# Plain instead of seven-fold products for one token block of the second expert, with a longer list of planner refinements

## The chip, the cores and the metric

One core of one Trainium2 chip. The metric is the device time of the kernel in microseconds (us). Before the change it is 1051.25 us, the median of three runs (1050.07 to 1051.81). The engines are named as in the profile: PE (TensorE, matmul), PEld (its weight loads), DVE (VectorE), ACT (ScalarE), POOL (GpSimd), SP (SyncE, which here issues the DMAs).

## The reference, cut to what matters

```python
def reference(**kw):                          # all float32
    attn = _attn_ref(q, k, v, s)              # q, k, v: (4, 8, 576, 64), causal, with a position bias from s
    x = attn.transpose(0, 2, 1, 3).reshape(2304, 512)
    h = x @ moe_w_in                          # 512 -> 2048, first expert
    x = (h - np.tanh(h)) @ moe_w_out          # 2048 -> 512
    a, b = x @ moe2_w_a, x @ moe2_w_b         # 512 -> 1536 each, second expert
    return (a * b) @ moe2_w_out               # 1536 -> 512, output (2304, 512)
```

## The kernel before, in words

Three stages follow one another and overlap: attention, the first expert in nine token blocks of 256, and the second expert in five token blocks, the first of 256 tokens and four of 512.

Every float32 operand is split into two 16-bit halves (high and low), and a product of two operands is three matmuls: high by high, high by low, low by high (`PROD`).

The second expert has 2304 tokens, 512 inputs and 1536 = 6 x 256 = 12 x 128 hidden columns. There are two ways to compute a block:

- **Plain** (`l3_mm`, `l3_act`, `l4_mm`; only the block of 256 tokens before the change). For each of the 12 tiles f of 128 hidden columns, 12 matmuls give a, 12 give b, ACT scales b into a tile `th`, DVE multiplies a by it into `g`, the result is split into `ghl` (the high half is a copy on ACT, DVE or POOL, the low half an operation on DVE or POOL), and `l4_mm` accumulates three matmuls of 512 columns for each 128 tokens into the `acc` banks.
- **Seven** (`seven`, `seven_act`, `seven_out`; the four blocks of 512). For each of the 6 chunks of 256 columns the 2x2 block product over (input halves, token halves) is done by seven instead of eight smaller products: 84 matmuls of 256 columns for a and b together and 24 of 512 columns for the output. It needs sums of token operands, five per block (`b_sums`), and sums of weight parts, five per chunk for a and b together, 30 in all (`a_sums`). One sum is three additions and a split: three operations on DVE or POOL, one copy on ACT, DVE or POOL, one subtraction on DVE or POOL. The results of `a_sums` lie in the space of the first expert's weights (`w1`, through `a_place`), so they can't be made before the first expert has used those; they are read from `w2`, the second expert's split weights. The intermediate values of `a_sums` lie in the buffers named `xf`, of which there are two (`XF = 2`), given out strictly in the order of the program (fifo); one buffer serves two sums, so the 30 sums take 15 in turn, and the first result buffer of `b_sums` comes behind them in the same order.

`blocks2` says which chunks are seven: block and chunk are counted through (block x 6 + chunk), and a chunk of a 512 block is seven from the number `SEVEN` on. With `SEVEN = 6` all of block 1 is seven.

The order of the instructions on each engine is not written out by hand. All operations are first recorded with their dependencies, a price in ns (`cost`) and a due time (`due`); a list scheduler (`Plan.run`) then walks a modelled time, and each engine takes the ready operation with the earliest due time whose buffers are free. Where an operation may run on several engines (`either`), `best` compares the modelled end times, with the prices of DVE multiplied by `WV` (attention and first expert) or `WV2` (second expert) and those of POOL by `WP`. Before the final run, `refine` performs one step for each entry of `REFINE`: it runs the model, computes how late each operation could start (`backward`), and moves the due times part of the way towards that, with random shifts from a seed. The engines then execute each queue in the fixed order that results: an instruction that waits holds up all behind it on its engine.

One line of the profile, L544, stands for nearly every instruction, since all are recorded through one helper; they are told apart by their tiles. `h`, `qk`, `acc` and `pv` are PSUM banks (2, 3, 2 and 1 of them). `pv` is also used for small sums, among them that of `x2_cols`, whose result DVE writes to `y1` (named y in the profile).

Of the kernel before, what the change touches and what calls it, by code (L numbers as in the profile page):

```python
# [3 lines left out]

# [29 lines left out]
MASKED = -1.0e34  # L34
BLOCKS = [(p, [b]) for p in range(2) for b in range(4)]
TURN = 0.0
REFINE = [(200.0, 0.2, 300.0, 242), (200.0, 0.2, 1000.0, 199), (0.0, 0.1, 0.0, 21), (100.0, 0.0, 1000.0, 484), (100.0, 0.05, 0.0, 139), (200.0, 0.2, 1000.0, 988), (400.0, 0.05, 300.0, 648), (0.0, 0.0, 1000.0, 437), (0.0, 1.0, 300.0, 81)]
SEVEN = 6
SUMSTEP = 20e3
XF = 2  # L40
WS = 2
# [3 lines left out]
PART1 = 60e3  # L45
TAILS = 100e3
SLACK = 0.0
WV = 1.1
WP = 1.2
WV2 = 1.1  # L50
N = None
ORDER1 = [7, 6, 5, 4, 7, 6, 5, 7, 6, 7, 6, N, N, N, N, N]
ORDER2 = [8, 7, 6, 5, N, N, 8, 7, 6, N, N, 8, 7, 8, N, N, N, N]
# [126 lines left out]


class Op:
    __slots__ = ("eng", "fn", "dur", "dl", "succ", "wait", "ready", "bufs", "seq", "lag", "size", "what", "alts", "done", "pred", "end", "part", "cost", "lock")


class Plan:
# [52 lines left out]
    def record(self, eng, fn, reads, writes, keys_r, keys_w, dur, lag, size, shift=0.0, alts=None):  # L239
        for part in (self.parts, self.alts):  # L240
            if part is not None:
                part.append((eng, fn, reads, writes, keys_r, keys_w, dur, lag, size, shift))
                return
        op = Op()
        op.eng, op.fn, op.dur, op.dl = eng, fn, dur, self.due + shift
        op.part = self.due, eng == "sync"
        op.cost = self.cost
        op.succ, op.wait, op.ready, op.seq = [], 0, 0.0, len(self.ops)
        op.lag, op.size = lag, size
        op.alts, op.done = alts or [(eng, fn, dur, lag)], False  # L250
        op.what = getattr(fn, 'what', '')
        op.bufs = []
        before = set()
        for kind, views in (("r", reads), ("w", writes)):
            for v in views:
                b = v.buf
                m = v.mask()
                assert kind == "w" or not b.fresh, b.name
                b.fresh = False
                if b not in op.bufs:  # L260
                    op.bufs.append(b)
                for p0, p1, hm, ho in b.wrote:
                    if hm & m and p0 < v.p1 and v.p0 < p1 and ho is not op:
                        before.add(ho)
                if kind == "r":
                    b.seen.append((v.p0, v.p1, m, op))
                    continue
                rest = []
                for h in b.seen:
                    p0, p1, hm, ho = h  # L270
                    if hm & m and p0 < v.p1 and v.p0 < p1:
                        if ho is not op:
                            before.add(ho)
                        if not hm & ~m and v.p0 <= p0 and p1 <= v.p1:
                            continue
                    rest.append(h)
                b.seen = rest
                b.wrote = [h for h in b.wrote if h[2] & ~m or h[0] < v.p0 or h[1] > v.p1]
                b.wrote.append((v.p0, v.p1, m, op))
        for v in self.hold:  # L280
            if v.buf not in op.bufs:
                op.bufs.append(v.buf)
        self.hold = ()
        for k in keys_r:
            before.update(self.keys.get(k, []))
        for o in before:
            o.succ.append(op)
        op.pred = list(before)
        op.wait = len(before)
        for k in keys_w:  # L290
            self.keys.setdefault(k, []).append(op)
        self.ops.append(op)

    def begin(self):

        self.open = {}
        self.unused = {}
        for t in self.tags.values():
            t["next"] = t["live"] = 0
        seen = set()  # L300
        for op in self.ops:
            op.wait, op.ready, op.done = len(op.pred), 0.0, False
            for b in op.bufs:
                if b not in seen:
                    seen.add(b)
                    b.left, b.real = 0, None
                    self.unused[b.pool] = self.unused.get(b.pool, 0) + 1
                b.left += 1
# [70 lines left out]
    def run(self, switch=None):  # L379
# [4 lines left out]
        ready = {e: [] for e in engines}  # L384
# [5 lines left out]

        def offer(op):
            for a in op.alts:
                heapq.heappush(ready[a[0]], (op.dl, op.seq, op))

        def best(op, e):
            mine = [a for a in op.alts if a[0] == e][0]
            least = mine[2] * op.cost.get(e, 1.0) + (max(port - now, 0.0) if mine[1].lock else 0.0)
            for a in op.alts:
                if a is not mine:
                    t = max(free[a[0]] - now, 0.0, port - now if a[1].lock else 0.0) + a[2] * op.cost.get(a[0], 1.0)  # L400
                    for dl, seq, o in ready[a[0]]:
                        if dl < op.dl and len(o.alts) == 1:
                            t += o.dur
                    if t < least:
                        return None
            return mine
# [12 lines left out]
        n = 0  # L419
        while left:  # L420
            moved = True
            while moved:
                moved = False
                for e in order():
                    if free[e] > now or not ready[e]:
                        continue
                    put, op = [], None
                    late = False
                    while ready[e]:
                        x = heapq.heappop(ready[e])  # L430
                        if x[2].done:
                            continue
                        way = x[2].alts[0] if len(x[2].alts) == 1 else best(x[2], e)
                        if way and self.fits(x[2], switch):
                            if not way[1].lock or port <= now:
                                op = x[2]
                                break
                            late = True
                        put.append(x)
                        if len(put) > 200:  # L440
                            break
                    for x in put:
                        heapq.heappush(ready[e], x)
                    if op is None:
                        if late:
                            n += 1
                            heapq.heappush(events, (port, n + 0.7, 1, None))
                        continue
                    for b in op.bufs:
                        if b.real is not None:  # L450
                            continue
                        t = self.tags[b.pool, b.tag]
                        t["live"] += 1
                        t["next"] = max(t["next"], b.nth + 1)
                        b.real = switch is None or self.open[b.pool].tile(
                            b.shape, b.dtype, tag=b.tag, name=b.name, bufs=t["bufs"])
                    op.eng, op.fn, op.dur, op.lag = way
                    op.done = True
                    op.lock = op.fn.lock
                    if op.lock:  # L460
                        port = now + op.dur
# [10 lines left out]
                    if e == "sync":  # L472
                        dma = max(dma, now + op.dur + 650.0) + op.size
                        end = dma
# [12 lines left out]
            now, _, kind, op = heapq.heappop(events)  # L487
            batch = [(kind, op)]
            while events and events[0][0] <= now:
                _, _, kind, op = heapq.heappop(events)  # L490
# [33 lines left out]
class _Eng:  # L524
# [3 lines left out]
    def __getattr__(self, what):  # L528
        plan, name = self.plan, self.name

        def call(*args, reads=(), writes=(), **kw):
            rd, wr = [], []
            for i, a in enumerate(args):
                if isinstance(a, View):
                    (wr if i == 0 else rd).append(a)
            for k, a in kw.items():
                if isinstance(a, View):
                    (wr if k in ("out", "accum_out") else rd).append(a)
            def real(a):
                assert not isinstance(a, View) or a.buf.real is not None, (name, what, a.buf.name, a.buf.tag)  # L540
                return a.real() if isinstance(a, View) else a

            def fn():
                getattr(getattr(plan.nc, name), what)(  # L544
                    *[real(a) for a in args], **{k: real(a) for k, a in kw.items()})

            fn.what = (name, what)
            fn.lock = shares(name, what, rd, wr)
            dur, lag, size = cost(name, what, rd, wr, kw, args)
            plan.record(name, fn, rd, wr, reads, writes, dur, lag, size, plan.shift.get(name, 0.0))  # L550

        return call
# [72 lines left out]
def tile_attention_two_moes(  # L625
# [22 lines left out]
    NF2 = F2 // P  # L648
# [974 lines left out]
    pl.vector.tensor_scalar(out=y2, in0=y1, scalar1=fin, scalar2=2.0 ** 43, op0=ALU.mult, op1=ALU.mult)  # L1623
    t0 = start[-1]
    todo = blocks2()
    t1 = t0 + NF2 * 36 * todo[0]["n"] / 2.4
    for i, c in enumerate(dict.fromkeys(c for blk in todo for c in blk["seven"])):
        due(t1 + (i - 3) * SUMSTEP)
        a_sums(c)
# [69 lines left out]
```

## Time and profile before

| | before |
|---|---|
| median of three runs | 1051.25 us |
| the profiled execution's own time | 1052.22 us |
| its span | 1050.4 us |
| PE busy | 922.6 us, 88% |
| DVE busy | 876.7 us, 83% |
| ACT busy | 545.1 us, 52% |
| POOL busy | 129.2 us, 12% |
| mean granted PE clock | 0.967 |

The span is the time from the first to the last instruction of the profiled execution; 1.8 us of that execution's own time lie around it. Busy times are shares of the span; an engine can bound one stretch and idle in another, so the stretches have to be looked at one by one. Of the granted clock, 1.00 is 2.4 GHz and 0.50 is 1.2 GHz.

### The profile page before, as it was taken

How to read it: one execution, taken by the hardware profiler on the slowest of the kernel's cores; microseconds unless marked ns; L12 is line 12 of the kernel's file. 1: busy time of each engine (PE TensorE's matmuls, PEld its weight loads, DVE VectorE, ACT ScalarE, POOL GpSimd, SP SyncE). 2: the span in 40 equal slices, each digit the busy share in tenths (PEclk: the TensorE clock that was granted, in tenths of full speed). 3: DMA queues.
4: the chain of work that ended last, by engine and by line, in shares of the span. 5: the costliest groups of instructions: out<-in, count | busy, mean ns of one | idle time of the engine just before them, and what ended most of it. 6: DMA issues, size and time to landing. Idle time of an engine off the chain costs nothing.

```text
span 1050.4 us, 21289 instructions
## 1 busy us (share of the span) xinstructions
PE 922.6 (88%) x8214; PEld 715.1 (68%) x8214; DVE 876.7 (83%) x2178; ACT 545.1 (52%) x1106; POOL 129.2 (12%) x194
## 2 busy tenths in 40 slices
PE   1698689997998989998898898169999999999998
PEld 0476578885777667777787785057777777777775
DVE  8899899798998999996999899999569559655555
ACT  6797766667777677874967443222222222212211
POOL 3120411013322332510000010000000000000000
PEclk9999899999999999999899998679999999999999
DMA  9999756378997988957735310010011002001001
GB/s 240 236 287 231 186 126 105 50 157 161 190 182 143 179 168 161 188 125 170 295 121 161 101 41 1 0 51 31 2 41 41 1 1 80 1 1 42 1 1 41
DMA packets 282086, 113.98 MB, mean 109 GB/s; under 512 B 251200, under 2 KB 265776, under 8 KB 281984
## 3 DMA queue, kind: packets, MB, share of 16 engines
q1 hardware_dynamic: 281984, 112.62, 46.3%
q8 instruction: 64, 1.05, 0.4%
q14 instruction: 38, 0.31, 0.1%
HBM read 60.53 MB, written 11.17 MB: 68 GB/s over the span
## 4 chain that ended last, share of the span: by engine, by line
PE 35%; DVE 14%; DMA 5%; ACT 3%; issue 1%; SPq 0%; DVEq 0%; ACTq 0%
PE h L544 13%; PE qk L544 9%; PE acc L544 8%; PE pv L544 5%; DVE xf L544 5%; DVE w L544 2%; ACT w L544 2%; DMA xf<-in_moe_w_out_dram 1%; DMA xhl<-x_d 1%; DVE ghl L544 1%; DVE x2f L544 1%; DVE x2hl L544 1%; DMA w<-in_moe_w_b_dram 1%; DVE g L544 1%; DMA w<-in_moe_w_a_dram 1%
## 5 line engine op out<-in xcount | busy, mean ns | idle before, releaser
L544 PEld LDWEIGHTS <-w 128*128 128x128 f16 x5376 | 526.2, 99 | 147.7 <-issue 33.1
L544 PE MATMUL h<-xhl,w 128*128 128x256 f16 x2256 | 281.4, 276 | 1.0 <-DVE xhl L544 1.0
L544 PE MATMUL acc<-ghl,w 128*128 128x256 f16 x1536 | 195.1, 277 | 9.9 <-DVE ghl L544 3.8
L544 PE MATMUL h<-xf,w 128*128 128x256 f16 (+1 forms) x704 | 103.6, 297 | 1.8 <-DVE w L544 1.5
L544 DVE TENSOR_TENSOR g<-g,h 128x512 f32<-128x512 f32 x48 | 32.8, 684 | 51.6 <-PE h L544 50.7
L544 DVE CUSTOM_DVE_ANT_0 qk<-qk,caus,cs 128x384 f32<-128x384 f32 (+2 forms) x120 | 64.4, 554 | 5.0 <-PE qk L544 4.6
L544 ACT ACTIVATE qk<-qk,nm 128x384 f32<-128x384 f32 (+2 forms) x120 | 59.8, 498 | 15.8 <-DVE nm L544 9.3
L544 PE MATMUL qk<-qkT 128*128 128x128 f16 (+4 forms) x168 | 46.8, 320 | 23.4 <-DVE a L544 14.0
L544 PEld LDWEIGHTS <-qkT 128*128 128x128 f16 (+2 forms) x352 | 29.3, 103 | 54.7 <-issue 32.4
L544 DVE SCALAR_TENSOR_TENSOR a<-qk,sm,a 128x384 f16<-128x384 f32 (+3 forms) x120 | 62.9, 547 | 4.0 <-ACT a L544 3.9
L544 PEld LDWEIGHTS <-ghl 128*128 128x128 f16 x360 | 35.2, 98 | 39.2 <-DVE ghl L544 2.7
L544 ACT ACTIVATE th<-pv 128x256 f32<-128x256 f32 x24 | 9.2, 383 | 94.9 <-PE pv L544 89.8
L544 ACT ACTIVATE sq<-h 128x512 f32<-128x512 f32 x48 | 28.5, 595 | 56.9 <-PE h L544 55.4
L544 ACT ACTIVATE th<-h,xc 128x512 f32<-128x512 f32 x64 | 43.8, 684 | 25.2 <-PE h L544 23.8
L544 ACT ACTIVATE ghl<-h,xsg 128x512 f16<-128x512 f32 x57 | 39.1, 685 | 30.0 <-DVE h L544 28.9
L544 DVE SCALAR_TENSOR_TENSOR h<-h,xc,th 128x512 f32<-128x512 f32 x64 | 48.1, 752 | 7.3 <-ACT th L544 6.9
L544 PE MATMUL acc<-w,ghl 128*128 128x512 f16 x216 | 52.1, 381 | 2.2 <-DVE ghl L544 2.2
L544 PEld LDWEIGHTS <-sq 128*128 128x128 f16 (+1 forms) x306 | 29.7, 98 | 35.0 <-POOL sq L544 2.0
L544 DVE SCALAR_TENSOR_TENSOR ghl<-h,xsg,ghl 128x512 f16<-128x512 f32 x64 | 47.5, 743 | 3.1 <-ACT ghl L544 2.9
L544 PE MATMUL qk<-kB,qkT 67*128 67x128 f16 (+4 forms) x168 | 46.3, 318 | 1.7 <-DMA kB<-part_d 1.6
L544 PEld LDWEIGHTS <-v 128*64 128x64 f16 x1440 | 37.8, 112 | 14.0 <-issue 13.4
L544 ACT ACTIVATE sq<-raw 128x576 bf16<-128x576 f32 (+2 forms) x57 | 38.6, 678 | 15.1 <-DMA raw<-tail_d 6.8
(243 smaller groups left out, 1683.5 us busy)
## 6 DMA issues: line engine op xcount, KB each, us to landing
w<-in_moe_w_out_dram SPq DMA_DIRECT2D x8, 1024.0 KB
w<-in_moe_w_in_dram SPq DMA_DIRECT2D x6, 1024.0 KB
x_d<-x2hl SPq DMA_DIRECT2D x18, 256.0 KB
raw<-in_k_dram SPq DMA_DIRECT2D x32, 128.0 KB
raw<-in_v_dram SPq DMA_DIRECT2D x32, 128.0 KB
w<-in_moe_w_a_dram SPq DMA_DIRECT2D x4, 1024.0 KB
xhl<-x_d SPq DMA_DIRECT2D x4, 1024.0 KB
out_dram<-x2f SPq DMA_DIRECT2D x16, 256.0 KB
```

The costliest lines, as they stand in the source:

```text
L544: getattr(getattr(plan.nc, name), what)(*[real(a) for a in args], **{k: real(a) for k, a in kw.items()})
```

## The change

Block 1 of the second expert becomes plain (`SEVEN` goes from 6 to 12), so blocks 2 to 4 are seven. The due times of the weight sums are moved behind all plain blocks together, where they lay behind block 0. The weights of DVE in the choice between engines rise (`WV` 1.1 to 1.3, `WV2` 1.1 to 1.2). `REFINE` has 26 steps where it had 9, none of them kept. The planner's ready queues become sorted lists in place of heaps, with the same order of due time and number, and its prices are rounded to whole ns.

```diff
-REFINE = [(200.0, 0.2, 300.0, 242), (200.0, 0.2, 1000.0, 199), (0.0, 0.1, 0.0, 21),
...
+REFINE = [(2000.0, 0.1, 300.0, 180), (2000.0, 0.2, 0.0, 123), (2000.0, 0.1, 300.0, 60),
...
-SEVEN = 6
+SEVEN = 12
...
-WV = 1.1
+WV = 1.3
 WP = 1.2
-WV2 = 1.1
+WV2 = 1.2
...
         def offer(op):
             for a in op.alts:
-                heapq.heappush(ready[a[0]], (op.dl, op.seq, op))
+                insort(ready[a[0]], (op.dl, op.seq, op))
...
                     for dl, seq, o in ready[a[0]]:
-                        if dl < op.dl and len(o.alts) == 1:
-                            t += o.dur
+                        if dl >= op.dl or t >= least:
+                            break
+                        if len(o.alts) == 1:
+                            t += o.alts[0][2]
...
-            dur, lag, size = cost(name, what, rd, wr, kw, args)
+            dur, lag, size = map(round, cost(name, what, rd, wr, kw, args))
...
     todo = blocks2()
-    t1 = t0 + NF2 * 36 * todo[0]["n"] / 2.4
+    t1 = t0 + NF2 * 36 / 2.4 * sum(blk["n"] for blk in todo if not blk["seven"])
     for i, c in enumerate(dict.fromkeys(c for blk in todo for c in blk["seven"])):
         due(t1 + (i - 3) * SUMSTEP)
         a_sums(c)
```

## Rows read from the trace of the kernel before

**Rows 1.** The page: busy time of each engine, and PE and DVE in 40 slices.
```profile
PE 922.6 (88%) x8214; PEld 715.1 (68%) x8214; DVE 876.7 (83%) x2178; ACT 545.1 (52%) x1106; POOL 129.2 (12%) x194
...
PE   1698689997998989998898898169999999999998
...
DVE  8899899798998999996999899999569559655555
```

**Rows 2.** Busy time by stretch: length, engines (instructions), granted clock, DMA.
```profile
45.00:140.00 95.00, 73.79 (x441) 57.56 (x441) 88.35 (x265) 74.34 (x144) 22.80 (x27) 0.95 0.95 243
140.00:250.00 110.00, 105.10 (x1045) 88.27 (x1042) 99.70 (x314) 72.92 (x180) 16.74 (x33) 1.00 0.57 110
250.00:480.00 230.00, 208.22 (x2574) 164.62 (x2573) 213.37 (x627) 174.11 (x387) 63.94 (x106) 0.99 0.88 166
480.00:605.50 125.50, 112.86 (x1046) 96.63 (x1040) 111.28 (x251) 79.53 (x107) 9.79 (x8) 0.95 0.51 168
605.50:660.00 54.50, 51.31 (x386) 38.66 (x383) 53.02 (x98) 21.17 (x42) 2.53 (x2) 0.93 0.06 20
660.00:690.40 30.40, 0.04 (x2) 0.03 (x2) 30.40 (x53) 8.71 (x14) 0.00 (x0) 0.57 0.00 0
690.40:789.00 98.60, 98.04 (x732) 72.58 (x733) 75.16 (x136) 25.24 (x47) 2.59 (x3) 0.98 0.11 33
...
877.00:963.00 86.00, 85.94 (x647) 63.18 (x646) 57.23 (x100) 20.14 (x38) 0.00 (x0) 1.00 0.04 13
```

**Rows 3.** PE in order of time: start, length, instructions, idle time before and releaser.
```profile
643.30 1.20 PE L544 MATMUL acc<-w,ghl 128*128 128x512 f16 x4 [2.25 <-DVE ghl L544]
645.43 2.72 PE L544 MATMUL pv<-xhl,w 128*128 128x256 f16 x12 [0.94 <-DVE bits L544]
647.95 2.77 PE L544 MATMUL h<-xhl,w 128*128 128x256 f16 x12
650.51 1.64 PE L544 MATMUL acc<-w,ghl 128*128 128x512 f16 x6
...
690.38 2.74 PE L544 MATMUL pv<-xhl,w 128*128 128x256 f16 x12 [30.36 <-DVE y L544]
693.68 2.22 PE L544 MATMUL pv<-xhl,w 128*128 128x256 f16 x12 [0.56 <-ACT th L544]
695.74 1.47 PE L544 MATMUL h<-xhl,w 128*128 128x256 f16 x12
697.05 1.46 PE L544 MATMUL acc<-w,ghl 128*128 128x512 f16 x6
698.34 1.47 PE L544 MATMUL h<-xf,w 128*128 128x256 f16 x12
```

**Rows 4.** DVE in order of time, around the end of the weight sums.
```profile
684.49 1.88 DVE L544 SCALAR_TENSOR_TENSOR w<-xf,w 128x512 f16<-128x512 f32 x3
686.29 0.68 DVE L544 SCALAR_TENSOR_TENSOR xf<-x2hl,xf 128x512 f16<-128x512 f32 x1
...
690.11 0.21 DVE L544 TENSOR_SCALAR y<-pv,xik 128x2 f32<-128x2 f32 x1
```

**Rows 5.** Groups of DVE instructions from 597 to 690 us: busy, mean ns, idle before.
```profile
L544 DVE TENSOR_TENSOR xf<-w 128x512 f32<-128x512 f16 x60 | 38.8, 679 | 0.0
L544 DVE TENSOR_TENSOR xf<-xf 128x512 f32<-128x512 f32 x30 | 20.3, 678 | 0.0
L544 DVE SCALAR_TENSOR_TENSOR w<-xf,w 128x512 f16<-128x512 f32 x29 | 19.4, 679 | 0.0
```

**Rows 6.** Windows of 10 us: the last of the gap.
```profile
680.00:690.00 10.00, 0.00 (x0) 0.00 (x0) 10.00 (x18) 2.87 (x5) 0.00 (x0) 0.50 0.00 0
```

**Rows 7.** Groups from 640 to 730 us: a 512-column scaling on ACT, a multiplication on DVE.
```profile
L544 ACT ACTIVATE bits<-h,cpc 128x512 f32<-128x512 f32 x2 | 1.4, 687 | 1.3 <-PE h L544 1.3
L544 DVE TENSOR_TENSOR bits<-h,bits 128x512 f32<-128x512 f32 x2 | 1.4, 680 | 0.0
```

**Rows 8.** Groups of DVE instructions up to 605 us: the largest group of copies.
```profile
L544 DVE TENSOR_SCALAR a<-qk,sm 128x512 f16<-128x512 f32 x13 | 9.7, 743 | 0.0
```

More of the change, by code (lines that the diff above doesn't have):

```diff
@@ L1 @@
 import heapq
+from bisect import bisect_left, insort
 import random
@@ L36 @@
 TURN = 0.0
-REFINE = [(200.0, 0.2, 300.0, 242), (200.0, 0.2, 1000.0, 199), (0.0, 0.1, 0.0, 21), (100.0, 0.0, 1000.0, 484), (100.0, 0.05, 0.0, 139), (200.0, 0.2, 1000.0, 988), (400.0, 0.05, 300.0, 648), (0.0, 0.0, 1000.0, 437), (0.0, 1.0, 300.0, 81)]
-SEVEN = 6
+REFINE = [(2000.0, 0.1, 300.0, 180), (2000.0, 0.2, 0.0, 123), (2000.0, 0.1, 300.0, 60), (100.0, 0.0, 300.0, 89760), (2000.0, 0.05, 300.0, 21221), (100.0, 0.3, 0.0, 973), (100.0, 0.05, 0.0, 783), (2000.0, 0.3, 2000.0, 579), (0.0, 0.1, 300.0, 477), (-200.0, 0.0, 300.0, 45834), (0.0, 0.1, 1000.0, 331), (0.0, 0.1, 1000.0, 12795), (2000.0, 0.05, 300.0, 56244), (-200.0, 0.1, 300.0, 44216), (0.0, 0.7, 2000.0, 938), (0.0, 0.1, 2000.0, 6594), (-200.0, 0.0, 1000.0, 66042), (200.0, 0.5, 1000.0, 11562), (200.0, 0.2, 0.0, 26092), (100.0, 0.2, 1000.0, 96071), (400.0, 0.1, 0.0, 92832), (-200.0, 0.05, 2000.0, 89277), (400.0, 0.0, 3000.0, 30568), (200.0, 0.05, 2000.0, 84539), (100.0, 0.05, 300.0, 64962), (-200.0, 0.1, 0.0, 21270)]
+SEVEN = 12
 SUMSTEP = 20e3
@@ L182 @@
 class Op:
-    __slots__ = ("eng", "fn", "dur", "dl", "succ", "wait", "ready", "bufs", "seq", "lag", "size", "what", "alts", "done", "pred", "end", "part", "cost", "lock")
+    __slots__ = ("eng", "fn", "dur", "dl", "succ", "wait", "ready", "bufs", "seq", "lag", "size", "what", "alts", "pred", "end", "part", "cost", "lock")
 class Plan:
@@ L249, in record @@
         op.lag, op.size = lag, size
-        op.alts, op.done = alts or [(eng, fn, dur, lag)], False
+        op.alts = alts or [(eng, fn, dur, lag)]
         op.what = getattr(fn, 'what', '')
@@ L301, in begin @@
         for op in self.ops:
-            op.wait, op.ready, op.done = len(op.pred), 0.0, False
+            op.wait, op.ready = len(op.pred), 0.0
             for b in op.bufs:
@@ L426, in run @@
                         continue
-                    put, op = [], None
+                    op = None
                     late = False
[L429 to L432, printed above, removed]
+                    for x in ready[e][:201]:
                         way = x[2].alts[0] if len(x[2].alts) == 1 else best(x[2], e)
@@ L438, in run @@
                             late = True
[L439 to L443, printed above, removed]
                     if op is None:
@@ L448, in run @@
                         continue
+                    for a in op.alts:
+                        del ready[a[0]][bisect_left(ready[a[0]], (op.dl, op.seq))]
                     for b in op.bufs:
@@ L457, in run @@
                     op.eng, op.fn, op.dur, op.lag = way
-                    op.done = True
                     op.lock = op.fn.lock
```

## The prediction, made before the changed kernel was run

> **What bounds the kernel now.** I read the page's busy shares and slices first. No engine is full over the span: PE 88%, DVE 83%. But PE's slices show one hole, a 1 followed by a 6 at about 656 to 710 us, while DVE's slices there are all 9 [rows 1]. The windows put it exactly: from 660.0 to 690.4 us PE does nothing (0.04 us) and DVE is busy for all 30.40 us. Before it, from 45 to 605.5 us, DVE is busy for 512.7 of 560.5 us and PE for 500.0; behind it PE is full, 98.04 of 98.60 us in block 1 and 85.94 of 86.00 in a later block, with DVE at 57 of 86 [rows 2]. So there are three regimes: DVE and PE close together up to 605, DVE alone from there to the end of the hole, PE alone from there on.
>
> The view of PE in order of time tells what ends the hole: 30.36 us before the matmuls into `pv` at 690.38, released by DVE's y [rows 3]. That is `y1`, at 690.11 on DVE, behind the weight sums and the first token sums of block 1 [rows 4]. It waits for no data: `x2_cols` was done long before. It is only placed late in DVE's queue. The deeper cause is what stands in front of it: from 597 to 690 us DVE does 60 + 30 + 29 = 119 operations of `a_sums`, with no idle time before any of them [rows 5]. Three of them in a row start 1.80 us before the next one, 0.60 us each [rows 4], so they take 119 x 0.60 = 71.4 us. Block 1 can't begin without them: its `b_sums` result lies in an `xf` buffer, and the fifo gives it out after the 15 of the weight sums. Had `y1` come early, PE would have finished block 0 and then waited all the same.
>
> **The change part by part.** The sum is made against the profiled execution (1052.22 us, span 1050.4); the median is 1.0 below that execution, and I apply the difference to the median.
>
> *The hole.* Plain block 1 needs neither `a_sums` nor `b_sums`, so PE can go from block 0 straight into it. Gone: 30.36 us, and the 0.56 us of the next wait [rows 3]; 30.9 us.
>
> *The clock behind the hole.* In the last 10 us of the hole the granted clock is 0.50, the lower level, 1.2 GHz [rows 6]. The first two groups of 12 matmuls behind it take 2.74 (against 1.47) and 693.68 to 695.74 = 2.06 us (against 695.74 to 697.05 = 1.31) [rows 3]: 1.27 + 0.75 = 2.0 us, gone too.
>
> *The small stall ahead of it.* At 640 to 650 us PE waits 2.25 us for a `ghl` and 0.94 us for `bits`, both from a DVE full of sums, and its next 24 matmuls run slow: 645.43 to 650.51 = 5.08 against 2.62 us [rows 3]. Together 5.65 us. The sums' due times now lie behind both plain blocks, so they should step back behind `ghl`. But DVE takes whatever is ready, and the model may still let a sum go first. Bounds 0 and 5.65; I take half, 2.8 us.
>
> *More matmul work in block 1.* 12 matmuls of 256 columns take 1.31 us, 0.109 each; 6 of 512 take 697.05 to 698.34 = 1.29 us, 0.215 each [rows 3]. Seven: a chunk is 84 x 0.109 + 24 x 0.215 = 14.3 us, six are 86.0 (the later block of rows 2 shows 85.94). Plain: 12 tiles x 36 x 0.215 = 92.9 us. Added, all of it on PE's path: 6.9 us. Nothing hides it, since PE is the bound from here on.
>
> *Block 1's own chain.* A plain tile needs a scaling on ACT (0.69), a multiplication on DVE (0.68) [rows 7], a copy and a subtraction, each like these: about 2.7 us. PE has the next tile's 24 matmuls of 512 columns meanwhile, 5.2 us, with `h`, `g` and `ghl` double. I cost it at nothing; without that cover it would be 2.7 us for each of 12 tiles, 32 us.
>
> *Are the sums done in time for block 2?* They are moved and not removed; the fifo of `xf` means that block 2 needs all 30 before its `b_sums`. From 605.5 us on DVE has 83.4 us of work that it did up to 690.4 [rows 2], 12 tiles x (2 x 0.60 + a copy of at most 0.60) = 21.6 for the plain block, 20 x 0.60 = 12.0 for the `b_sums` of block 2, and I allow 10 for what stood behind the hole (`y1`, the last split, the output of block 0): 127 us. PE has the 51.3 us that it did between 605.5 and 660 [rows 2] and 92.9 of plain block, 144 us. So the sums are hidden, with some 17 us to spare, and what comes next is limited by PE, as block 2 is already. If that cover is gone, the `b_sums` stand open: 12 us. SP's queue has little in it here (DMA share 0.06 and 0.11 in these stretches [rows 2]); block 2's tokens are loaded when block 0 gives back its buffer, long ahead.
>
> This cover hangs on the 0.60 us. The Trainium skill (VectorE: DVE Perf Modes, "The DRAIN you can't avoid") says that the next operation on DVE doesn't start before the pipe of the one ahead is empty. Taken at its word, a sum's operation costs its full 0.68 us [rows 5], and 163 operations would add 13 us: 140 of 144, hardly any cover left. The trace has starts 0.60 apart with lengths of 0.68 to 0.69 [rows 4], so a tail of 0.08 us overlaps; the measurement decides, and the sum above stands.
>
> *Everything before 605 us.* New refinement steps, `WV` 1.3 and rounded prices reorder every queue there. None of this removes work; PE's work up to 605 us is unchanged. What it can win is idle time: 60.5 us on PE, 47.8 us on DVE from 45 us on, with ACT idle for 159.6 of 560.5 us [rows 2]. `WV` pushes copies towards ACT; the largest group of such copies on DVE has 9.7 us [rows 8], and DVE is the fuller engine. Bounds: a third of PE's idle time at best, -20 us; on the other side a plan that is worse by as much as one small stall in each of two places, +11. I take -6, a tenth of PE's idle time. From 605.5 on, `WV2` touches only a DVE that is not the bound.
>
> Sum: -30.9 - 2.0 - 2.8 + 6.9 - 6 = -34.8, from 1051.25 to 1016.4; I say 1016 us.
>
> **The rivals.**
> (a) The order before 605 us wins far more, 15 to 20 us: 1002 to 1007. For it: ACT's 160 idle us and DVE's lead. Against: DVE is at 91% there, and PE at 89%, both must be fed at once.
> (b) It loses up to 11 us: up to 1033. For it: the whole order is drawn anew, by a model and not by this trace.
> (c) Block 2 waits for its token sums: 1016 + 12 = 1028. For it: the fifo. Against: 17 us of spare.
> (d) The hole stays: `y1` is again queued behind the sums, since the new due times are as free to put it there. Then nothing but -6 and +6.9 is left: 1052. Against: the sums now have later due times, and plain tiles behind `pv` give the model a price for a late `y1`, which it hadn't while block 1 waited anyway.
> (e) Slower: the hole is cut up and spread. In block 1 each of the 12 tiles needs DVE twice, in a queue that is full of sums. Where a tile's `ghl` comes late, as at 640 us, PE stands and then runs at 1.2 GHz: 5.65 us a time, of which 2.46 is clock [rows 3]. All 12 tiles: 12 x 5.65 = 67.8, 1084 us; from seven such stalls on (7 x 5.65 = 39.6 against 34.8) the kernel is slower than before. For it: DVE is over 97% busy from 605.5 to 660 [rows 2]. Against: in that same stretch PE was busy for 51.31 of 54.5 us [rows 2] with block 0, whose tiles have half the matmuls for cover. The Trainium skill (TensorE: Matmul & The Clock Gate, "HAM oscillation") describes this, a clock lost again at each repeated wait, so that many short gaps can cost more than one long one; the stall at 640 us agrees, 3.19 us of waiting followed by 2.46 us of slow matmuls.
>
> **How the numbers follow.** Forecast 0.58, with its own range 1007 to 1026; (a) 0.13; (b) 0.12; (c) 0.09; (d) 0.04; (e) 0.04. (a), (b) and (c) are faster like the forecast, 0.92; I count (d) half as no change and half as slower: 0.92 faster, 0.02 same, 0.06 slower. A difference below 0.2% (2.1 us) can't be told from none. The range takes in (c), nearly all of (b) and most of (a): 1001 to 1033.
>
> **What would show it.** Right: no PE idle time over 5 us between 600 and 1000 us; the granted clock at 0.9 or more in each window of 10 us from 610 on; block 1 as 12 x 36 matmuls of 512 columns in about 93 us; weight sums on DVE beside them, the last of them before block 1 ends; the three seven blocks at 86 us each. The part before 605 us is right if the point that is at 605.5 us in the windows before (where the last weights of the second expert are split and its first matmuls start) comes between 592 and 604 us. Wrong: a wait of PE for `y`, `ghl` or token sums of 10 us or more in total behind 605; or a start of the second expert that moves by more than 15 us either way.

## The result, and the profile after

| | before | after |
|---|---|---|
| median (lowest to highest) | 1051.53 us (1050.07 to 1054.76), 4 runs | 1019.39 us (1017.87 to 1020.79), 4 runs |
| profiled execution: time, span | 1052.22, 1050.4 us | 1020.0, 1018.2 us |
| mean granted PE clock | 0.967 | 0.987 |

The ratio is 0.969, with a 95% interval of 0.9663 to 0.9717: 32 us faster. 1016 us was predicted, with a range of 1001 to 1033.

The page of the changed kernel, busy time of each engine and the slices of PE and DVE; it answers to [rows 1].
```profile
PE 921.8 (91%) x7998; PEld 691.8 (68%) x7998; DVE 831.4 (82%) x2084; ACT 546.7 (54%) x1101; POOL 140.9 (14%) x201
...
PE   1688789998877888899999999999999999999998
...
DVE  7799999879989999999799999999456659545554
```
The 1 and the 6 in PE's slices are gone: from the 18th slice on (433 us), each but the last is a 9. DVE's busy time fell by 45 us and PE's by 0.8, so PE's share rose to 91% by the shorter span alone.

Windows of the changed kernel: length, then busy time (instructions) of PE, weight loads, DVE, ACT, POOL, granted clock, DMA share, GB/s. The first six have the bounds of [rows 2]; then come the rest of block 1, the first seven block, and all behind 605.5 us.
```profile
45.00:140.00 95.00, 76.70 (x455) 60.65 (x454) 86.91 (x265) 79.67 (x149) 15.56 (x21) 0.93 0.87 229
140.00:250.00 110.00, 104.05 (x1035) 87.03 (x1033) 94.88 (x298) 74.83 (x184) 20.59 (x31) 1.00 0.61 119
250.00:480.00 230.00, 199.14 (x2422) 156.59 (x2423) 215.04 (x599) 159.36 (x354) 69.32 (x108) 0.97 0.87 161
480.00:605.50 125.50, 120.63 (x1212) 104.82 (x1211) 114.18 (x271) 92.16 (x135) 10.97 (x10) 1.00 0.59 180
605.50:660.00 54.50, 52.90 (x418) 40.32 (x416) 54.43 (x109) 23.21 (x47) 2.42 (x2) 1.00 0.07 20
660.00:690.40 30.40, 30.40 (x142) 13.81 (x141) 30.39 (x52) 10.75 (x19) 1.16 (x1) 1.00 0.22 70
690.40:746.00 55.60, 55.60 (x259) 25.25 (x258) 35.27 (x60) 10.29 (x16) 0.00 (x0) 1.00 0.00 1
746.00:832.00 86.00, 85.78 (x644) 62.71 (x642) 52.61 (x93) 21.57 (x40) 6.22 (x5) 1.00 0.08 26
...
605.50:1018.20 412.70, 406.21 (x2796) 272.89 (x2793) 282.83 (x500) 109.67 (x200) 16.55 (x14) 1.00 0.07 24
```
The stretch from 660.0 to 690.4, in which PE did nothing [rows 2], is full on PE *and* on DVE. The last line is everything behind 605.5 us; the same view of the kernel before reads:
```profile
605.50:1050.40 444.90, 406.91 (x3032) 298.38 (x3029) 324.79 (x569) 113.99 (x213) 7.11 (x6) 0.96 0.07 22
```
These two lines hold the result. The stretch is shorter by 444.9 - 412.7 = 32.2 us, the whole difference of the spans (1050.4 - 1018.2), as it must be when both are cut at the same moment; what tells is what fills it. PE's idle time in it falls from 38.0 to 6.5 us, by 31.5; its busy time hardly moves (-0.7). From 45 to 605.5 us PE's idle time is 60.5 us before [rows 2] and, by the first four windows above, 560.5 - 500.5 = 60.0 after.

PE in order of time in the changed kernel (start, length, instructions, in brackets the idle time before and its releaser), answering to [rows 3]:
```profile
606.53 0.16 PE L540 MATMUL pv<-wac,ones 128*128 128x1 bf16 x1 [0.59 <-ACT xf L540]
...
610.66 2.67 PE L540 MATMUL acc<-ghl,w 128*128 128x256 f16 x23 [0.97 <-DVE ghl L540]
613.17 1.47 PE L540 MATMUL qk<-xhl,w 128*128 128x256 f16 x12
...
644.99 2.75 PE L540 MATMUL qk<-xhl,w 128*128 128x512 f16 x12
...
659.34 2.75 PE L540 MATMUL h<-xhl,w 128*128 128x512 f16 x12
...
704.67 2.75 PE L540 MATMUL qk<-xhl,w 128*128 128x512 f16 x12
707.26 2.75 PE L540 MATMUL h<-xhl,w 128*128 128x512 f16 x12
...
743.52 2.75 PE L540 MATMUL pv<-xhl,w 128*128 128x512 f16 x12
746.11 1.47 PE L540 MATMUL h<-xf,w 128*128 128x256 f16 x12
```
The first product of block 1 (512 columns, from `xhl`) starts at 644.99, between tiles of block 0; from 659.34 to the first product of block 2 at 746.11 no group has a bracket: no wait. The last outputs of block 0 fall into this stretch, and those of the last three tiles of block 1 behind it. Twelve such matmuls take 707.26 - 704.67 = 2.59 us, so block 1's 12 x 36 cost 36 x 2.59 = 93.2 us.

DVE in order of time in the changed kernel, answering to [rows 4], and its groups of the sums from 597 to 750 us, answering to [rows 5]:
```profile
646.45 0.21 DVE L540 TENSOR_SCALAR y<-pv,xik 128x2 f32<-128x2 f32 x1
...
701.90 0.69 DVE L540 SCALAR_TENSOR_TENSOR w<-xf,w 128x512 f16<-128x512 f32 x1
702.50 0.69 DVE L540 TENSOR_TENSOR g<-h,th 128x512 f32<-128x512 f32 x1
703.11 1.29 DVE L540 SCALAR_TENSOR_TENSOR w<-xf,w 128x512 f16<-128x512 f32 x2
704.31 0.69 DVE L540 SCALAR_TENSOR_TENSOR ghl<-g,ghl 128x512 f16<-128x512 f32 x1
...
705.51 0.69 DVE L540 SCALAR_TENSOR_TENSOR w<-xf,w 128x512 f16<-128x512 f32 x1
...
720.15 0.68 DVE L540 SCALAR_TENSOR_TENSOR w<-x2hl,w 128x512 f16<-128x512 f32 x1
```
```profile
L540 DVE TENSOR_TENSOR xf<-w 128x512 f32<-128x512 f16 x59 | 39.3, 701 | 0.0
L540 DVE SCALAR_TENSOR_TENSOR w<-xf,w 128x512 f16<-128x512 f32 x29 | 19.3, 685 | 0.0
L540 DVE TENSOR_TENSOR xf<-xf 128x512 f32<-128x512 f32 x29 | 19.2, 685 | 0.0
```
There are 117 operations of weight sums where there were 119: they are moved, not removed. The plain block's `g` and `ghl` now stand between them, one pair to a tile. The last weight sum is at 705.51, the last token sum of block 2 at 720.15, ended 25 us ahead of block 2's first product (746.11 - 720.83). And `y1` comes at 646.45, 44 us earlier.

### The profile page after: what moved, and what is told of

It reads as the page before. It is cut to its first block, busy times and chain, and to the rows that moved or that the text cites. A ratio compares the mean times of both kernels' runs of the same rounds, so it can differ in the third digit from the quotient of the medians.

```text
span 1018.2 us, 20791 instructions
## 1 busy us (share of the span) xinstructions
PE 921.8 (91%) x7998; PEld 691.8 (68%) x7998; DVE 831.4 (82%) x2084; ACT 546.7 (54%) x1101; POOL 140.9 (14%) x201
## 4 chain that ended last, share of the span: by engine, by line
PE 50%; DVE 23%; DMA 12%; ACT 8%; issue 5%; SPq 2%; POOL 0%; DVEq 0%; ACTq 0%; POOLq 0%
PE h L540 19%; PE acc L540 13%; PE qk L540 12%; PE pv L540 6%; DMA qkT<-qk 5%; DVE qk L540 4%; DVE a L540 3%; DVE w L540 3%; SPq L540 2%; ACT sq L540 2%; DVE g L540 2%; ACT w L540 2%; DVE h L540 1%; DVE ghl L540 1%; DMA w<-in_moe_w_in_dram 1%
## 5 line engine op out<-in xcount | busy, mean ns | idle before, releaser
L540 PEld LDWEIGHTS <-w 128*128 128x128 f16 x5160 | 500.8, 98 | 135.4 <-issue 28.3
L540 PE MATMUL h<-xhl,w 128*128 128x256 f16 (+1 forms) x2256 | 296.8, 283 | 7.0 <-DVE ghl L540 3.3
L540 PE MATMUL h<-xf,w 128*128 128x256 f16 (+1 forms) x560 | 85.9, 304 | 1.0 <-ACT xf L540 0.8
L540 ACT ACTIVATE qk<-qk,nm 128x384 f32<-128x384 f32 (+3 forms) x120 | 59.9, 499 | 35.9 <-DVE nm L540 23.6
L540 DVE CUSTOM_DVE_ANT_0 qk<-qk,caus,cs 128x384 f32<-128x384 f32 (+3 forms) x120 | 64.7, 555 | 4.0 <-PE qk L540 3.1
L540 PE MATMUL acc<-w,ghl 128*128 128x512 f16 x252 | 60.6, 379 | 0.0
L540 ACT ACTIVATE sq<-h 128x512 f32<-128x512 f32 x36 | 21.4, 596 | 60.2 <-PE h L540 58.7
L540 DVE TENSOR_TENSOR g<-sq 128x256 f32<-128x256 f32 x35 | 14.4, 422 | 47.4 <-ACT sq L540 47.3
L540 ACT ACTIVATE w<-w 128x1024 f32<-128x1024 f32 (+1 forms) x42 | 48.2, 1158 | 6.4 <-DMA w<-in_moe_w_a_dram 2.4
L540 DVE TENSOR_TENSOR g<-g,h 128x512 f32<-128x512 f32 x36 | 24.5, 685 | 27.4 <-PE h L540 26.2
```

The costliest lines, as they stand in the source:

```text
L540: getattr(getattr(plan.nc, name), what)(*[real(a) for a in args], **{k: real(a) for k, a in kw.items()})
```

## Experiments

Each ratio is against the kernel before, run on the same chip. Two theories stand against each other. *The hole*: the sums that block 1 needs, 71 us of DVE work, are what PE waited for, and the plain block is what removes the wait. *The order*: the hole is an accident of one queue (`y1` behind the sums), and the refined order, not the plain block, is what removes it.

### One part at a time, each with its old or new plan

**e1_block_alone**: the plain block in the kernel before; its refinement steps, weights and planner stay.
```diff
-SEVEN = 6
+SEVEN = 12
-    t1 = t0 + NF2 * 36 * todo[0]["n"] / 2.4
+    t1 = t0 + NF2 * 36 / 2.4 * sum(blk["n"] for blk in todo if not blk["seven"])
```


> The kernel before with block 1 plain and the sums' due times behind it, with its old planner, old weights and old 9 refinement steps. Theory (the hole goes because a plain block needs no sums): no PE wait over 5 us behind 600 us, 30 us less than before, 1021 us, give or take 8 since the 9 steps were drawn for another order. Rival (the gain is the new order: 26 steps, new weights): at least half of the 32 us stay lost, 1035 us or more.

Measured: 1086.0 us, ratio 1.0348 (1.0293 to 1.0403), slower. PE in order of time, around its longest wait:
```profile
678.08 1.47 PE L544 MATMUL qk<-xhl,w 128*128 128x256 f16 x12
698.74 1.87 PE L544 MATMUL acc<-w,ghl 128*128 128x512 f16 x4 [19.18 <-ACT x2f L544]
```
And ACT's queue in that wait:
```profile
689.86 1.23 ACT L544 ACTIVATE w<-xf 128x512 f16<-128x512 f32 x2 [1.78 <-DVE xf L544]
...
693.20 0.63 ACT L544 ACTIVATE x2hl<-x2f 128x512 f16<-128x512 f32 x1 [2.10 <-DVE x2f L544]
...
698.09 0.60 ACT L544 ACTIVATE x2f<-acc 128x512 f32<-128x512 f32 x1 [4.26 <-DVE x2hl L544]
```
The first theory missed; the other's bound, 1035 us or more, is met, but by a hole of which it said nothing. This hole is there although no matmul of block 1 needs a sum: the `acc` banks that block 0 needs still hold the first expert's last result, and the operation that empties them (`x2f<-acc`) stands in ACT's fixed queue behind copies of sums, and these wait for DVE, one after the other. That is rival (d)'s mechanism with another releaser. Much of the loss lies ahead of 605.5 us, where PE is busy for 493.1 us against 515.7 in the kernel before. The likely reason, not shown apart, is that the nine steps were drawn for another program.

**e2_plan_alone**: the changed kernel with the seven block 1; of the 26 steps, nine, in which the planner's model finds no order with this block, are skipped.
```diff
-SEVEN = 12
+SEVEN = 6
...
```


> The changed kernel with block 1 seven again, so the new planner, weights and refinement steps alone (9 of the 26 steps, after which the model can no longer place every operation, are left out). Theory: the hole stays, PE waits 25 to 40 us for the sums at the start of block 1, 1051 us give or take 8. Rival (the new order does it): 1030 us or less and a hole under 10 us.

Measured: 1093.56 us, ratio 1.0419 (1.0379 to 1.0459). PE's waits behind 595 us (in total, times, longest):
```profile
PE acc L546 <- ACT x2f L546: 35.5, 1, 35.5
```
A hole stays, as the first theory said, but its releaser is that of e1, in which block 1 is plain; so it does not speak for that theory. The time is far above what either theory gave, again with steps drawn for another program.

**e9_no_refine**: the changed kernel without any step.
```diff
-REFINE = [(2000.0, 0.1, 300.0, 180), (2000.0, 0.2, 0.0, 123), (2000.0, 0.1, 300.0, 60),
...
+REFINE = []
```


> The changed kernel without any refinement step (due times as recorded). What the steps are worth: if they only trim (theory so far: 6 us ahead of 605 us and a part of the small stalls), 1019 + 10 = 1029 us, and no hole, since block 1 is plain. If it is they that keep the evacuations ahead of the sums in the queues, as the run of the block alone suggests (19 us for x2f), a wait of 10 us or more for x2f, y or bits, and 1045 us or more.

Measured: 1061.55 us, ratio 1.0103 (1.0068 to 1.0139). No PE wait behind 595 us is longer than 2.2 us, so the plain block has no hole without refinement either; both forecasts missed, the one by its time, the other by its wait. The span is 44.6 us longer than the changed kernel's (1062.8 against 1018.2). Of these, 23.7 are idle time of PE ahead of 605.5 us, 19.0 of them in two stretches; 8.0 are idle time behind, and 12.9 are longer busy time for the same matmuls, at a mean granted clock of 0.976 against 0.987:
```profile
45.00:140.00 95.00, 68.83 (x411) 55.07 (x411) 87.88 (x257) 72.56 (x136) 9.79 (x13) 0.92 0.86 226
480.00:560.00 80.00, 65.53 (x701) 51.67 (x699) 68.29 (x178) 54.13 (x89) 4.00 (x8) 0.94 0.74 182
```
In each of the two the changed kernel has PE busy for 76.70 us.

**e5_y_early**: the kernel before, with `y1`'s due time put ahead of everything for the final run.
```diff
+        early.append(len(pl.ops))
         pl.vector.tensor_scalar(
...
         pl.refine(REFINE)
+        for i in early:
+            pl.ops[i].dl = -1e9
```


> The kernel before, with y1 put ahead of all else on DVE in the last run of the planner (due time moved far forward, nothing else). Theory (block 1 waits for the sums whatever y1 does): PE finishes block 0 some 20 us sooner and then waits for the token sums; 1046 to 1052 us. Rival (the late y1 is the cause of the hole, as the wait's releaser says): 1021 us or less.

Measured: 1047.88 us (10 runs), ratio 0.9977 (0.9952 to 1.0001). PE in order of time:
```profile
663.40 1.47 PE L544 MATMUL h<-xhl,w 128*128 128x256 f16 x12
664.71 2.85 PE L544 MATMUL acc<-w,ghl 128*128 128x512 f16 x12
689.66 0.37 PE L544 MATMUL h<-xf,w 128*128 128x256 f16 x1 [22.10 <-ACT xf L544]
```
`y1` is no longer waited for, PE finishes block 0, and then waits 22.1 us for the first token sums instead. The releaser that the trace named for the 30.36 us [rows 3] was only the last in a queue; taking it away is worth about 3 us, at the edge of what the runs can tell. That tells against the theory of the accident: with `y1` early (at 648.4 us) the token sums alone hold PE.

**e4_token_sums_first**: the kernel before, with block 1's token sums recorded behind the first chunk's weight sums, so that the fifo of `xf` gives them the fourth buffer and not the sixteenth (the five sums of a chunk take three).
```diff
-    for i, c in enumerate(dict.fromkeys(c for blk in todo for c in blk["seven"])):
-        due(t1 + (i - 3) * SUMSTEP)
-        a_sums(c)
+    chunks = list(dict.fromkeys(c for blk in todo for c in blk["seven"]))
+    due(t1 - 3 * SUMSTEP)
+    a_sums(chunks[0])
...
             b_sums(blk, j % 2)
+            for i, c in enumerate(chunks):
+                if i and j == 1:
+                    due(t1 + (i - 3) * SUMSTEP)
+                    a_sums(c)
```


> The kernel before (block 1 seven), with the token sums of block 1 recorded right behind the weight sums of the first chunk, so that they take their xf buffer third in the row and not sixteenth. If the fifo alone makes the hole: it goes without any added matmul work, about 33 us less, 1018 us. If the amount of DVE work binds too (158.6 us of it were done between 605.5 and 789, all of it needed by the end of block 1): the hole is cut up into waits in block 1, block 1 ends no earlier than 605.5 + 158.6 = 764 (now 784), at most 20 us less, 1031 us or more.

Measured: 1092.42 us, ratio 1.041 (1.0369 to 1.0451), with one long wait of PE:
```profile
708.11 2.74 PE L544 MATMUL pv<-xhl,w 128*128 128x256 f16 x12 [34.34 <-DVE y L544]
```
The time says nothing: recording the sums elsewhere upset the whole order, and the second expert starts over 40 us later. But the wait is the mirror of e5. The token sums of block 1 are all done by 699.2 us, and PE still stands, in block 0, until `y1` at 707.8, which is queued behind weight sums. So the place in the fifo alone does not remove the hole either.

### The same, with the order ahead of the sums held

In e1, e2 and e4 an edit of what lies behind 605 us upset what lies ahead of it. So the next kernels hold one kernel's modelled placement for all operations that its model starts before the first weight sum: their engine is fixed, they aren't ready before their time (`at`), they go first, and refinement leaves them alone. The rest is planned anew with 1 to 8 steps chosen for each kernel, so that these kernels differ in their steps too.
```diff
+        for op in pl.ops[:m]:
+            if on[op.seq] < 5:
+                op.at, op.fixed, op.dl = float(at[op.seq]), True, float(at[op.seq]) - 1e7
+                op.alts = [a for a in op.alts if a[0] == ("tensor", "vector", "scalar", "gpsimd", "sync")[on[op.seq]]]
...
-            op.wait, op.ready = len(op.pred), 0.0
+            op.wait, op.ready = len(op.pred), op.at
```

**h1_before_order_plain**: the kernel before, its placement held, with e1's edit. **h2_after_order_seven**: the changed kernel, its placement held, with `SEVEN = 6`.

> Block 1 plain, with the sums' due times behind it; the modelled placement of the kernel before is held for every operation that starts ahead of the first weight sum (so nothing before about 600 us is drawn anew), and only the rest is planned, with one refinement step chosen for it. Theory (a plain block frees PE from the sums): no PE wait over 5 us behind 605 us, no gain ahead of it: 1051 - 30.9 - 2.0 - 2.8 + 6.9 = 1022, within 6. Rival (nearly all of the 32 us is the new order ahead of 605 us, a plain block is worth nothing by itself, as the run of the block alone at 1086 us suggests): 1045 us or more.

> The reverse: the changed kernel's placement is held for all that starts ahead of the first weight sum, block 1 is seven again, and the rest is planned with six refinement steps chosen for it. Theory: PE stands for 20 to 35 us before block 1, released by token sums or by something queued behind the weight sums; 1019 + 30.9 + 2.0 - 6.9 = 1045, within 8. Rival (the order does it): 1025 us or less.

Measured: h1 1040.0 us, ratio 0.9894 (0.9853 to 0.9934); h2 1056.7 us (9 runs), ratio 1.0052 (1.003 to 1.0075). PE's longest wait in h1:
```profile
620.92 1.46 PE L554 MATMUL h<-xhl,w 128*128 128x256 f16 x6 [5.73 <-DVE wsc L554]
```
PE and DVE in h2:
```profile
686.94 2.74 PE L550 MATMUL pv<-xhl,w 128*128 128x256 f16 x12 [37.39 <-DVE y L550]
```
```profile
682.43 2.52 DVE L550 SCALAR_TENSOR_TENSOR w<-xf,w 128x512 f16<-128x512 f32 x4
...
686.64 0.25 DVE L550 TENSOR_SCALAR y<-pv,xik 128x2 f32<-128x2 f32 x1
```
The mechanism of the first theory holds in both: plain with the old order has no hole (its longest wait is for the split of the second expert's weights, at the seam of the held part), seven with the new order has it, 37.4 us long. Both times are above the forecast; h1's lies between that of the theory (1022) and that of the rival (1045). In h1 the seam costs: PE is busy for 34.46 of the 45.5 us ahead of 605.5, against 39.21 in the kernel before, and by 605.5 us it has done 98 matmuls fewer of the first expert, at 0.109 us each some 11 us.

**h5_after_order_tokens_first**: h2's edit together with e4's. (h3, the same edits with eight other steps, has no time: the order that came of them deadlocks.)

> The changed kernel's placement held for all that starts ahead of the first weight sum, block 1 seven, and its token sums recorded right behind the weight sums of the first chunk, so that they come third and not sixteenth in the fifo of xf; eight refinement steps chosen for the rest. If the place in the fifo makes the hole: PE waits less than 10 us in all behind 605 us and the kernel is at 1019 - 6.9 = 1012, up to 1022. If the amount of DVE work makes it: waits of 15 us or more in block 1 for the sums of later chunks, 1028 us or more (DVE has 158.6 us of work from 605.5 to the end of block 1, against 138 of PE).

Measured: 1021.96 us (5 runs), ratio 0.9729 (0.97 to 0.9758); the changed kernel run again beside it (**after_again**) 1018.85 us, ratio 0.969 (0.9663 to 0.9718). Windows of h5:
```profile
605.50:660.00 54.50, 48.55 (x388) 37.53 (x386) 54.13 (x107) 23.42 (x44) 2.64 (x2) 1.00 0.09 27
660.00:690.00 30.00, 27.40 (x216) 20.95 (x215) 29.22 (x49) 10.73 (x23) 7.04 (x6) 1.00 0.16 54
690.00:765.00 75.00, 72.88 (x548) 53.34 (x546) 74.32 (x126) 27.35 (x49) 16.03 (x11) 1.00 0.05 15
```
DVE in order of time, the first token sum and `y1`:
```profile
625.68 0.69 DVE L551 SCALAR_TENSOR_TENSOR xf<-x2hl,xf 128x512 f16<-128x512 f32 x1
...
633.75 0.21 DVE L551 TENSOR_SCALAR y<-pv,xik 128x2 f32<-128x2 f32 x1
```
This is the run that names the cause. Block 1 is seven and needs its sums, all made by the same DVE, and yet there is no hole; block 1 takes the weight sums as they come. Two things stand early that stood behind the sums in h2: the token sums, by their place in the fifo, and `y1`, 53 us earlier, by the planner. With `y1` alone early PE waits 22.1 us for token sums (e5), with the token sums alone early 34.3 us for `y1` (e4). So the hole is the place of both behind the weight sums. What remains is the amount: DVE is full up to 765 us, and PE loses 5.95, 2.60 and 2.12 us in these windows, 10.7 in all, a little more than the 10 expected, in waits of at most 2.4 us. That eats the 6.9 us of matmul work that seven saves.

> The changed kernel unaltered, as the yardstick on the same chip for the other runs of this group: 1019 us, within 2.

**h4_after_order_seven10** and, the same kernel again beside after_again, **h4_again**: the placement of the changed kernel held, the last two of block 1's six chunks seven.
```diff
-SEVEN = 12
+SEVEN = 10
...
```


> The changed kernel's placement held ahead of the sums, and the last two of the six chunks of block 1 seven (the first four plain), four refinement steps chosen for the rest. Theory (17 us or more of cover are left in block 1): the sums are done in time for the last two chunks, PE has 2 x 1.15 = 2.3 us less to do and waits for nothing new: 1017 us. Rival (the cover was just enough): the token sums of two blocks now stand in block 1, PE waits for them, 1021 us or more.

> The kernel with the last two chunks of block 1 seven, again, beside the changed kernel on one chip: 2.3 us less matmul work, 2.3 us under the changed kernel if DVE's cover holds; equal to it if the difference of 3.4 us between the two groups of runs was the chip's.

Measured: 1016.01 us, ratio 0.967 (0.9641 to 0.9699), and 1016.22 us, ratio 0.9669 (0.9641 to 0.9697), 2.6 us below after_again on the same chip. PE's waits behind 595 us in h4_again, all of them:
```profile
PE acc L550 <- DVE p2b L550: 1.0, 1, 1.0
PE pv L550 <- ACT xf L550: 0.6, 1, 0.6
```
Two of six chunks give back a third of 6.9 us = 2.3, and nothing new waits. It is the best version of all, though the intervals of it and of the changed kernel overlap.

**h6_sums_due_early**: the changed kernel, its placement held, with the old due times of the weight sums.
```diff
-    t1 = t0 + NF2 * 36 / 2.4 * sum(blk["n"] for blk in todo if not blk["seven"])
+    t1 = t0 + NF2 * 36 * todo[0]["n"] / 2.4
...
```


> The changed kernel's placement held for all that starts ahead of the first weight sum, block 1 plain, but the sums' due times as they were, behind block 0 alone; three refinement steps chosen (on the new due times) for the rest. This is the one line of the change not yet undone by itself. Theory (DVE takes the sums whenever it is free, and block 1 is plain): no wait over 3 us, 1019 us within 3. Rival (the later due times are what keeps the sums behind the block's own work): stalls of PE for ghl or y like those at 640 us before, 5.65 us each, 1027 us or more.

Measured: 1028.44 us (6 runs), ratio 0.9788 (0.9754 to 0.9821). PE in order of time:
```profile
610.33 0.27 PE L550 MATMUL acc<-ghl,w 128*128 128x256 f16 x1 [2.39 <-ACT ghl L550]
611.53 4.18 PE L550 MATMUL acc<-ghl,w 128*128 128x256 f16 x23 [0.93 <-DVE ghl L550]
617.48 0.60 PE L550 MATMUL pv<-sq,ones 128*128 128x256 bf16 x4 [1.78 <-ACT sq L550]
...
622.07 2.72 PE L550 MATMUL pv<-xhl,w 128*128 128x256 f16 x12 [2.68 <-DVE bits L550]
```
With the old line the kernel is about 9 us slower (1028.44 against 1019.39): with early sums PE waits four times within 12 us, twice for ACT and twice for DVE, 7.8 us in all, and the matmuls behind two of these waits run slow (4.18 us for 23, where the changed kernel has 2.67 in the same place). The theory, that the line makes no difference once the block is plain, is wrong; the rival's bound, 1027 us or more, is met. How much of the 9 us is due to the three new steps was not tried apart; in h4 a held placement with new steps cost nothing. The hole doesn't come back, so it isn't this line that removes it.

`WV`, `WV2` and the rounding of prices were not tried each by itself.

## Why the prediction was right, and where it was off

The forecast's sum was -34.8 us on the profiled execution; the spans differ by 32.2.

**The hole, -30.9: right.** PE's idle time behind 605.5 us fell by 31.5, and its longest wait there is 1.0 us. The reason holds too: e5 shows that a wait for token sums stood behind the wait for `y1`, and h5 that with both early there is no hole. The prediction's words that block 1 "can't begin without" all weight sums are true of that order only, and it did not say that `y1` alone can hold PE as long, as e4 shows.

**The clock behind it, -2.0: right.** The granted clock is 1.00 in each stretch from 605.5 on.

**The small stall, -2.8: right in size, too cautious in reason.** The 5.65 us at 640 to 650 are gone; the changed kernel has 2.5 us of waits elsewhere behind 605.5, with no slow matmuls, which leaves -3.1. But I bounded the due-time line by the stall that was there, 0 to 5.65; h6, in which the changed order lacks it and three steps are new, has four waits and is about 9 us slower.

**More matmul work, +6.9: right**: 93.2 us for block 1 against the 86.0 that I had for a seven block, +7.2 (the 86 us behind 746.0 hold 644 of such a block's 648 matmuls); h4's 2.6 us for a third of it agrees.

**Block 1's own chain, 0: right**, no wait in 659 to 746 us.

**The sums beside it: right, with more room.** From the last token sum to block 2's first product there are 25 us, where I had 17 to spare. I had put all 12 plain tiles ahead of the token sums; four of them come behind. Starts on DVE are 0.60 us apart again (701.90, 702.50, 703.11) with lengths of 0.69. At its full length each operation would have cost 0.08 more, 13 us in all by the prediction's count. The Trainium skill (VectorE: DVE Perf Modes, "The DRAIN you can't avoid"), which the prediction quoted for the full length, adds in the same place that an operation that is not held starts earlier; the starts here agree with that.

**Ahead of 605.5 us, -6: this term was mis-sized.** PE's busy time behind 605.5 moved by -0.7, of which +7.2 is the plain block and -4.5 the slow clock (2.0, and 2.46 at 640 us [rows 3]); -3.4 are left over. Most of that is work already done: by 605.5 us PE has done 1534 of the first expert's matmuls into `h`, 1512 before, and as many into `acc` (1488); 22 at 0.109 us are 2.4 us. The rest would be slow matmuls that the sum left out. So some 2.4 us were won ahead, against the 6 of the forecast. Idle time there, on which I had counted, did not fall: 60.5 and 60.0 us. With as much busy time (515.7 and 515.6 us) more work was done, because matmuls ran less often slow; in the kernel before, a single group close ahead of the cut is slow by as much:
```profile
600.69 5.07 PE L544 MATMUL acc<-ghl,w 128*128 128x256 f16 x23 [0.92 <-DVE p2a L544]
```
The same 23 matmuls take 2.67 us in the changed kernel (at 610.66, above). That the forecast of this term had the right sign is luck: it counted on idle time. Nor is the order a small extra: without steps the loss is 43 us (e9), and the two halves of the change don't add.

| | block 1 seven | block 1 plain |
|---|---|---|
| order of before ahead of the sums | 1051.5 (before) | 1040.0 (h1) |
| order of after ahead of the sums | 1056.7 (h2) | 1019.4 (after) |

The plain block is worth 11.5 us in the one order and 37.3 in the other, and the new order costs 5 us without the plain block and gives 20.6 with it. How much of h1's distance is the seam of the held part, and how much the old order itself, is left open.

**The marker was wrong.** I said the second expert would start between 592 and 604 us. Its first matmuls come at 613.17, 8 us later than before, although PE had done 2.4 us more of its work: the first expert is finished wholly before the second begins, where they were interleaved. A place in a queue was a poor measure of progress; the number of matmuls done by a fixed moment is a better one.

**The rivals.** (a) and (b): what lies ahead moved by 2.4 us, not by 11 or 15. (c): 25 us to spare. (d) did not happen, but e1 shows how near it was: the plain block with the old steps kept a wait of 19 us. (e) did not happen: twelve tiles, no stall; h6 has two stalls of its kind.

## What to carry to other kernels

When PE waits for an operation at the end of an in-order queue, ask what stands in front of it and what else stands behind the same work: moving the named releaser alone gave about 3 us (e5), moving the token sums alone left a wait of 34.3 us for the releaser (e4); with both early (h5), or with `y1` early and no token sums needed (the change), the wait of 30 us is gone. Giving the bound engine a little more work (6.9 us) was right since it let 70 us of another engine's work run beside it; then give back as much of it as the cover allows (h4). In these runs an order found by search did not carry over to an edited program (e1, e2, e4): judge an edit by a plan made for it, or hold the part that it doesn't touch.

## What the runs showed that was not expected

Short waits that come close together cost clock as well: in h6 a wait of 2.39 and one of 0.93 us, 1.2 us apart, are followed by 23 matmuls that take 4.18 us instead of 2.67, and 617 to 625 us repeats it, with waits of 1.78 and 2.68 us and 12 matmuls of 2.72 us instead of 1.47; the granted clock is 0.94 over 605.5 to 660. The slow matmuls add some 2.8 us to 7.8 us of waiting. In the changed kernel waits of 0.59 and 0.97 us at the same place, 4 us apart, left it at 1.00. Whether it is the length of the waits or their distance that makes the difference, no run shows.
